# The first microseconds of a windowed attention and its feed-forward layer: masks, reciprocals and values prepared in another way, in another order

## The chip, the cores and the metric

The kernel runs on one core of a Trainium2 chip. A core has a matmul engine (TensorE, PE in the profile, with its weight loads shown apart as PEld), a vector engine (VectorE, DVE), an engine for functions of one operand (ScalarE, ACT), a general engine (GpSimd, POOL) and an engine that only issues transfers (SyncE, SP). Each engine works through its own instructions in the order in which they are written; between engines, semaphores make an instruction wait for its inputs and for the space of its output. 16 DMA engines move data between the memory of the chip (HBM) and the core's memory (SBUF); matmuls write to a second memory, PSUM, of eight banks.

The metric is the time of one execution on the chip, in microseconds (us), lower is better.

## The reference

```python
# q, k, v: 8 batches, 8 heads, 576 positions, 64 wide; w_in 512 x 2048, w_out 2048 x 512
scores = (q @ k.T) / 8
scores = np.where(abs(i - j) <= 32, scores, -1e9)     # a window of 65 keys
attn = np.exp(scores - scores.max(-1)); attn = attn / (attn.sum(-1) + 1e-9)
x = (attn @ v), heads side by side                     # 4608 tokens x 512
h = x @ w_in; g = np.maximum(0.01 * h, h)
out = g @ w_out
```

The maximum is not subtracted in the kernel, since the scores are small. The division by the sum is done after the product with v.

## The kernel before

**Steps.** Heads are taken in pairs: head 0 of a pair lies in partitions 0 to 63, head 1 in 64 to 127. A step is one pair `p` and one half `hf` of a batch `b`: 288 query positions. Step `i` has `b, hf, p = i // 8, (i // 4) % 2, i % 4`; there are 64. The keys are cut into nine blocks of 64 positions, and a half touches five of them (`WIN`, L134): scores come transposed, keys in partitions, queries along the free axis. Even and odd blocks are kept apart in two rows of 288, so that 2 x 288 scores stand in PSUM (`ps`).

A step is made of these parts: `score` (matmuls into ps), `exps` (ACT, L312, the exponential of all 576 columns, to `e` in bf16), `masked` (L320, e times a 0/1 mask on DVE or POOL, to `prob`), `sums` (L342, a matmul with `ones_bd`, which adds the keys of each head and gives the sum in all 64 partitions of that head), `inverse` (L352, reciprocal on DVE), `product` (L367 for batch 0, L375 for the others, prob with v, to `x` in PSUM) and `scaled` (L391, x times the reciprocal, to `xT` in bf16, which is laid out as the next matmul wants it). For batches 1 to 7 the two heads of a pair are put into the diagonal blocks of 128 x 128 matrices (`kbd`, `vbd`), the other blocks being zero, so that one matmul does both heads; vbd has two buffers, for even and odd batches, and the zeros are written once, in the loop of L664 to L668. For batch 0 each head has its own 64 x 64 matmul, from `v0b`.

**Groups.** The steps of one half of a batch (four pairs) make one group of 288 tokens. For it, the first feed-forward matmul (L405) makes 16 tiles `f` of 128 hidden units, each from four chunks `c` (one for each pair); ACT applies the leaky maximum (L416, Prelu) into `gT`. The second (L463) makes the output in tiles of 128 tokens.

**Order.** The order of all instructions is written by hand; a framework only adds the semaphores and the buffers of the tile pools. From batch 1 on, a planner (L716 to L754) spreads the steps between the matmuls of the feed-forward layer by due times. The opening, batch 0 with groups 0 and 1, is a list of calls (L537 to L673). There, `transpose_first` (L208) turns k and q by 18 matmuls for a pair, `evict_first` copies the result to SBUF (L143 on DVE, L141 on ACT), `h_chunk(c)` does chunk c of the first four tiles of group 0, `h_open(f)` does a whole tile f of it, `h_close(f)` is its Prelu. After the list comes group 1 (`h_first(1)`, then L665) and the transposes of batch 1.

In the list before, score(0) stands behind the transposes of k of pair 1. Masks 0 and 1 are made on DVE, 2 to 7 on POOL; every step has its `inverse` on DVE. score(1) to score(6) come ahead of h_chunk(0), score(7) after h_chunk(1).

**Buffers in PSUM.** `mmps` has four banks for everything called `mm` or `tp`: transposes and feed-forward tiles, used in turn. `ps` takes two banks, and `s` and `x` one each: a new score waits until exps has read the last, and so on.

**Masks.** `win` (128 x 128) holds the band of ones, made for each half of the partitions by two selections on POOL (L151, L155: a selection keeps elements where an affine function of partition and column is not negative, and fills the others with 0). `spread` copies it side by side into `wide`, from which the masks are read as overlapping views (`mask_at`).

**Loads.** k and q of batch 0 are loaded by POOL's DMA queue (L99), which converts f32 to bf16, for each pair in turn; v of pair 0 by SP and ACT in f32, then copied to v0b (`value_first`); v of the other pairs by POOL (L116), then w_in in four quarters (L529), w_out in four (L533), and k, q and v of batch 1. POOL issues each of them, which takes it 0.5 to 0.8 us, in one order with its own computations.

**Zero matmuls.** `keep_busy` (L475) issues matmuls of 224 columns of zeros, whose results nobody reads; 14 of them open the program.

Of the kernel before, what the change touches and what calls it, by code (L numbers as in the profile page):

```python
# [9 lines left out]
FP32 = mybir.dt.float32  # L10
# [6 lines left out]
def kernel(  # L17
# [14 lines left out]
    nc = tc.nc  # L32
# [71 lines left out]
    v0b = const.tile([128, NPAIR, NB, D], BF16, name="v0b")  # L104
# [4 lines left out]
    def load_v(b, p, engs=(nc.sync, nc.sync)):  # L109

        cast = engs[0] is nc.gpsimd
        if not cast:
            vf[b, p] = fload.tile([128, NB, D], FP32, name=f"vf{p}")
        for a, r in enumerate(HEADS):
            to = vf[b, p][r] if not cast else v0b[r, p] if b == 0 else vbd[b % 2][r, p, :, r]
# [12 lines left out]
    ident = const.tile([128, 128], BF16)  # L128
# [18 lines left out]
    win = const.tile([128, 128], BF16)  # L147
    nc.gpsimd.memset(win, 1.0)
    for lo in (0, 64):
        w = win[lo:lo + 64]  # L150
        nc.gpsimd.affine_select(  # L151
            out=w, in_=w, compare_op=ALU.is_ge, fill=0.0,
            base=0, channel_multiplier=-1, pattern=[[1, 128]],
        )
        nc.gpsimd.affine_select(  # L155
            out=w, in_=w, compare_op=ALU.is_ge, fill=0.0,
            base=2 * W, channel_multiplier=1, pattern=[[-1, 128]],
        )

# [23 lines left out]
    nc.vector.tensor_copy(out=ident, in_=ident_f)  # L183
# [36 lines left out]
    def value_first(b, p, eng):  # L220
        copy_to(eng, v0b[:, p], vf[b, p])
# [111 lines left out]
    def sums(i):  # L333

        b, hf, p = where(i)
        pr, both = probs[i][:2]
        s = xps.tile([128, HALF], FP32, name="s")
        if both is not None:
            nc.tensor.matmul(s, ones_bd, both, start=True, stop=True)  # L339
        else:  # L340
            for n in range(2):
                nc.tensor.matmul(  # L342
                    s, ones_bd, pr[:, n].rearrange("p c i -> p (c i)"),
                    start=(n == 0), stop=(n == 1),
                )
        probs[i][2] = s
        if b > 0:
            inverse(i)
# [5 lines left out]

    def product(i):
# [7 lines left out]
        if b == 0:  # L363
            for n_, blk, i0, n in parts:
                lo, hi = 2 * i0, 2 * (i0 + n)
                for r in HEADS:
                    nc.tensor.matmul(  # L367
                        x[r, lo:hi], v0b[r, p, blk], flat[r, n_, lo:hi],
                        start=(blk == parts[0][1]), stop=(blk == parts[-1][1]),
                        skip_group_check=True,  # L370
                    )
        else:
            for n_, blk, i0, n in parts:
                lo, hi = 2 * i0, 2 * (i0 + n)
                nc.tensor.matmul(  # L375
                    x[:, lo:hi] if b < NATURAL else x_v[:, :, i0:i0 + n], vbd[b % 2][:, p, blk, :],
                    flat[:, n_, lo:hi] if b < NATURAL else pr[:, n_, :, i0:i0 + n],
                    start=(blk == parts[0][1]), stop=(blk == parts[-1][1]),
                    skip_group_check=True,
                )  # L380
        probs[i][3] = x
# [6 lines left out]

    def scaled(i):
        r, x = probs.pop(i)[2:]  # L390
        nc.vector.tensor_mul(place(i), x, r)  # L391
# [145 lines left out]
    keep_busy(ps, 0, 14, True)  # L537
    fill(V)
    transpose_first(0, 0, "k")
    evict_first(0, 0, "k", V)  # L540
    transpose_first(0, 0, "q")
    evict_first(0, 0, "q", A)
    transpose_first(0, 1, "k")
    score(0)
    evict_first(0, 1, "k", V)
    spread(A, GAP + 32, 2)
    load_v(0, 1, (G, G))
    transpose_first(0, 1, "q")
    exps(0)
    value_first(0, 0, V)  # L550
    transpose_first(0, 2, "k")
    evict_first(0, 1, "q", A)
    spread(V, 0, 3)
    masked(0, V)
    load_v(0, 2, (G, G))
    transpose_first(0, 2, "q")
    evict_first(0, 2, "k", V)
    sums(0)
    evict_first(0, 2, "q", A)
    score(1)  # L560
    inverse(0)
    transpose_first(0, 3, "k")
    exps(1)
    load_v(0, 3, (G, G))
    transpose_first(0, 3, "q")
    evict_first(0, 3, "k", A)
    score(2)
    product(0)
    evict_first(0, 3, "q", A)
    load_w_in(0, 512)  # L570
    masked(1, V)
    exps(2)
    scaled(0)
    sums(1)
    load_w_in(512, 1024)
    score(3)
    inverse(1)
    product(1)
    masked(2, G)
    exps(3)  # L580
    score(4)
    masked(3, G)
    exps(4)
    scaled(1)
    sums(2)
    product(2)
    inverse(2)
    score(5)
    load_w_in(1024, 1536)
    exps(5)  # L590
    masked(4, G)
    score(6)
    scaled(2)
    sums(3)
    h_chunk(0)
    load_w_in(1536, 2048)
    exps(6)
    inverse(3)
    h_chunk(1)
    masked(5, G)  # L600
    score(7)
    product(3)
    h_chunk(2)
    load_w_out(0)
    scaled(3)
    sums(4)
    exps(7)
    h_chunk(3)
    inverse(4)
    masked(7, G)  # L610
    product(4)
    h_close(0)
    h_close(1)
    h_open(4)
    load_w_out(1)
    h_close(2)
    h_open(5)
    scaled(4)
    h_close(4)
    sums(5)  # L620
    masked(6, G)
    h_open(6)
    h_close(3)
    inverse(5)
    h_close(5)
    h_open(7)
    h_close(6)
    product(5)
    load_w_out(2)
    h_close(7)  # L630
    h_open(8)
    h_open(9)
    load_w_out(3)
    h_close(8)
    scaled(5)
    sums(6)
    h_close(9)
    h_open(10)
# [3 lines left out]
    load_first(1, 2, "q", 2)  # L642
    inverse(6)
    product(6)
    h_close(10)
    h_open(11)
# [3 lines left out]
    h_close(12)  # L650
    scaled(6)
    sums(7)
    h_close(13)
    h_open(14)
    inverse(7)
    h_open(15)
    h_close(14)
# [125 lines left out]
```

## Time and profile before

| | us |
|---|---|
| median of 3 runs | 315.69 (315.33 to 316.57) |
| the profiled execution, its own time | 316.52 |
| its span, first to last instruction | 314.8 |
| PE busy | 303.4 (96%) |
| DVE busy | 218.0 (69%) |
| ACT busy | 167.8 (53%) |
| POOL busy | 186.3 (59%) |
| mean granted clock of PE | 0.989 |

The span is what the profile shows; the execution's own time has 1.7 us around it. In the profile's lines, `out<-in` names the tile written and the tile read, `x` and a number is a count, and a bracket at the end of a line of the timeline gives the idle time before it and what ended it. The granted clock is the share of the full clock that PE was given. A transfer's time to landing counts from the start of its issue. "Releaser" is what a waiting instruction waited for last.

Some durations that the prediction uses, in us: reciprocal of 128x288 f32 on DVE 1.956; scaling (L391) 0.457; eviction of 128x576 on DVE 0.756, on ACT 0.650; exps 0.648; Prelu of 128x288 f32 (L416) 0.410; POOL's mask 1.27; DVE's mask 0.51 (median 0.459); memset of 128x576 words on DVE 0.538, of 128x1152 bf16 on POOL 1.108.

Landings of the opening's loads, from the view of transfers: k and q of pair 0 at 4.9 and 5.9, of pair 1 at 7.85 and 8.6, of pair 2 at 9.3 and 10.1, of pair 3 at 10.9 and 11.6; the quarters of w_in at 18.9, 21.5, 24.8 and 27.3, of w_out at 29.8, 32.7, 35.2 and 37.8; the first keys of batch 1 at 39.2.

### The profile page before, as it was taken

Reading aid. Unit: us, or ns where it says so; the run is one execution under the profiler, and the core shown is the slowest. Engines: PE = TensorE matmul, PEld = TensorE weight load, DVE = VectorE, ACT = ScalarE, POOL = GpSimd, SP = SyncE. Lnnn points to the kernel's source line nnn. Section 1 sums busy time; section 2 is a strip of 40 time slices with the busy share of each in tenths; the row PEclk is TensorE's granted clock in tenths of the full one; section 3 lists DMA queues with packets and bytes.
Section 4 is the critical chain, followed back from the end, with each engine's and each line's share of the span. In section 5 each row is a group of like instructions: output and inputs, shape, how many; then the busy total and the mean of one; then the engine's idle time right before and its main releaser. Section 6 shows DMA issues by size and latency. Waiting matters only on the chain.

```text
span 314.8 us, 6932 instructions
## 1 busy us (share of the span) xinstructions
PE 303.4 (96%) x2693; PEld 203.9 (65%) x2714; DVE 218.0 (69%) x268; ACT 167.8 (53%) x370; POOL 186.3 (59%) x257
## 2 busy tenths in 40 slices
PE   4889999999999999999999999999999999999996
PEld 3656755685856767585856758585765858576653
DVE  2889759899647996698655996688655997565100
ACT  2646655482825648282834828284652828364531
POOL 8989975606557855796466856786546866330000
PEclk9779999999999999999999999999999999999999
DMA  8999999969998994599627994699734620000102
GB/s 127 141 185 207 207 149 252 210 145 228 229 199 211 234 196 111 124 201 225 147 56 195 184 225 129 78 248 217 159 77 121 110 55 35 34 35 1 67 28 74
DMA packets 107313, 46.09 MB, mean 146 GB/s; under 512 B 68752, under 2 KB 102800, under 8 KB 107280
## 3 DMA queue, kind: packets, MB, share of 16 engines
q1 hardware_dynamic: 91936, 37.91, 57.9%
q0 software_dynamic: 14752, 7.59, 18.3%
q8 instruction: 21, 0.34, 0.5%
q10 hardware_dynamic: 592, 0.15, 0.2%
q14 instruction: 12, 0.10, 0.1%
HBM read 36.70 MB, written 9.44 MB: 147 GB/s over the span
## 4 chain that ended last, share of the span: by engine, by line
PE 93%; DVE 2%; DMA 2%; POOL 1%; issue 1%; ACT 0%; ACTq 0%; DVEq 0%; POOLq 0%
PE mm L405 40%; PE mm L463 39%; PE x L375 4%; PE ps L301 4%; PE s L339 2%; DVE r L352 2%; DMA qb<-in_q_dram 2%; PE s L342 1%; PE tp L208 1%; PE ps L293 1%; PE x L367 1%; POOL kb L99 0%; PE ps L284 0%; POOL qb L99 0%; ACT e L312 0%
## 5 line engine op out<-in xcount | busy, mean ns | idle before, releaser
L352 DVE RECIPROCAL r<-s 128x288 f32<-128x288 f32 x64 | 125.2, 1956 | 52.9 <-PE s L339 50.6
L405 PE MATMUL mm<-xT,w_in_bf 128*128 128x288 bf16 x1024 | 134.8, 287 | 0.1
L463 PE MATMUL mm<-w_out_bf,gT 128*128 128x512 bf16 (+2 forms) x571 | 129.8, 373 | 1.2 <-issue 0.2
L416 ACT ACTIVATE gT<-mm 128x288 bf16<-128x288 f32 x256 | 101.6, 410 | 26.2 <-PE mm L405 9.3
L405 PEld LDWEIGHTS <-w_in_bf 128*128 128x128 bf16 x1024 | 98.7, 98 | 25.5 <-issue 0.3
L320 POOL TENSOR_TENSOR prob<-e,mask 128x576 bf16<-128x576 bf16 x48 | 61.1, 1272 | 84.1 <-issue 40.2
L463 PEld LDWEIGHTS <-gT 128*128 128x128 bf16 x592 | 55.9, 98 | 57.7
L468 ACT ACTIVATE o_sb<-mm 128x512 f32<-128x512 f32 (+2 forms) x37 | 21.7, 586 | 90.3 <-PE mm L463 90.3
L312 ACT ACTIVATE e<-ps 128x576 bf16<-128x576 f32 x64 | 41.5, 648 | 17.6 <-PE ps L301 7.4
L391 DVE TENSOR_TENSOR xT<-x,r 128x288 bf16<-128x288 f32 x64 | 29.3, 457 | 7.6 <-PE x L367 0.6
L235 POOL CAST vbd<-vf 64x576 bf16<-64x576 f32 x48 | 33.0, 688 | 1.4
L262 DVE COPY kbd<-kT 64x576 bf16<-64x576 bf16 x48 | 32.0, 666 | 0.3
L230 POOL CAST kb<-kf 96x384 bf16<-96x384 f32 x48 | 27.3, 593 | 1.1 <-DMA kf<-in_k_dram 1.1
L230 POOL CAST qb<-qf 96x384 bf16<-96x384 f32 x48 | 24.6, 539 | 4.3 <-DMA qf<-in_q_dram 4.3
L375 PE MATMUL x<-prob,vbd 128*128 128x96 bf16 (+1 forms) x280 | 22.5, 211 | 0.0
L330 DVE TENSOR_TENSOR both<-prob 128x288 bf16<-128x288 bf16 x52 | 19.6, 376 | 0.8
L301 PEld LDWEIGHTS <-kbd 128*128 128x128 bf16 x240 | 15.5, 98 | 6.8
L375 PEld LDWEIGHTS <-vbd 128*128 128x128 bf16 x280 | 17.9, 98 | 2.3
L301 PE MATMUL ps<-qT,kbd 128*128 128x128 bf16 (+2 forms) x240 | 19.3, 211 | 0.0
L339 PE MATMUL s<-both,ones_bd 128*128 128x288 bf16 x52 | 14.9, 286 | 0.0
L320 POOL TENSOR_TENSOR prob<-e,wide 128x576 bf16<-128x576 bf16 x7 | 8.9, 1274 | 4.6 <-ACT e L312 4.5
L141 ACT ACTIVATE qT<-tp 128x576 bf16<-128x576 bf16 x7 | 4.4, 650 | 6.9 <-PE tp L208 6.9
(51 smaller groups left out, 108.7 us busy)
## 6 DMA issues: line engine op xcount, KB each, us to landing
out_dram<-o_sb SPq DMA_DIRECT2D x35, 256.0 KB, 3.7
vf<-in_v_dram SPq DMA_DIRECT2D x49, 144.0 KB, 3.3
qf<-in_q_dram SPq DMA_DIRECT2D x24, 288.0 KB, 4.4
kf<-in_k_dram SPq DMA_DIRECT2D x24, 288.0 KB, 4.7
w_in_bf<-in_moe_w_in_dram POOLq DMA_DIRECT2D x4, 512.0 KB, 8.3
w_out_bf<-in_moe_w_out_dram POOLq DMA_DIRECT2D x4, 512.0 KB, 9.3
kb<-in_k_dram POOLq DMA_DIRECT2D x4, 144.0 KB, 4.9
qb<-in_q_dram POOLq DMA_DIRECT2D x4, 144.0 KB, 5.1
```

Source lines behind the costliest of these rows:

```text
L230: nc.gpsimd.tensor_copy(out=dst[:, p, 3 * c:3 * c + 3], in_=by_c[c])
L235: nc.gpsimd.tensor_copy(out=vbd[b % 2][r, p, :, r], in_=vf[b, p][r])
L262: nc.vector.tensor_copy(out=to.rearrange("p n (m c) -> p n c m", c=2), in_=kT[r].rearrange("p (c n m) -> p n c m", c=2, n=NB),)
L301: nc.tensor.matmul(ps_v[:, n_, :, i0:i0 + n], kbd[b % 2][:, p, blk], by_c[:, :, hf * EVEN + i0:hf * EVEN + i0 + n], start=True, stop=True,)
L312: nc.scalar.activation(out=e, in_=ps[:, P0:P0 + 2 * HALF], func=AF.Exp, scale=scale)
L320: eng.tensor_mul(pr.rearrange("p n c i -> p n (c i)"), e.rearrange("p (n t) -> p n t", n=2), allowed,)
L352: nc.vector.reciprocal(r, probs[i][2])
L375: nc.tensor.matmul(x[:, lo:hi] if b < NATURAL else x_v[:, :, i0:i0 + n], vbd[b % 2][:, p, blk, :], flat[:, n_, lo:hi] if b < NATURAL else ...
L391: nc.vector.tensor_mul(place(i), x, r)
L405: nc.tensor.matmul(h[:, 0:HALF], w_in_bf[:, c, ts(f, 128)], xT[:, c, ds(g * HALF % RING, HALF)], start=(c == 0), stop=(c == DMC - 1),)
L416: nc.scalar.activation(out=to, in_=x, func=AF.Prelu, alpha=0.01)
L463: nc.tensor.matmul(o[:, lo:hi], gT[:, f, ds(128 * j % RING, 128)], w_out_bf[:, f, lo:hi], start=(f == 0), stop=(f == FFC - 1),)
```

## The change

It touches only the opening and what the opening shares with the rest.

1. `band` (128 x 192) takes the place of `win`. Two selections over all 128 partitions make a band from which head 0 reads columns 0 to 127 and head 1 columns 64 to 191; `spread` works on one head at a time. The ones are written by DVE. The identity is made in bf16 directly, its zeros by DVE.
2. For steps 0 to 3 the reciprocal 1/s is made as y = exp(-ln s) on ACT (`log_of`, `guess`) and one Newton step on DVE: `missed` makes s*y, `mended` makes (s*y - 2)*y, which is minus the reciprocal, and `scaled` multiplies by it and by -1. Steps 4 to 7 of batch 0 and all later ones keep the reciprocal of DVE. An ACT table set is named at the start of ACT's queue.
3. v of batch 0 goes into the diagonal blocks of vbd[0], and `product` uses 128 x 128 matmuls there too. vbd[0] is zeroed by DVE at the start; in the loop of group 1 POOL zeroes only vbd[1].
4. The zero matmuls at the start write a tile of mmps instead of ps, and nine more stand between the steps, into a tile `spare`. The sums of steps 1 and 2 go into tiles of mmps as well.
5. The list of the opening is ordered anew: score(0) before the transposes of pair 1, masks 2, 3 and 7 on DVE, evictions dealt out otherwise, three quarters of w_in and most of w_out issued before POOL's first mask, scores 5 to 7 after h_chunk(0).

The core of the diff. Of the old list only the head is shown; it is printed whole above.

```diff
     load_v(0, 0, (nc.sync, nc.scalar))
+    nc.scalar.preload_act_table_set("natural_log_exp_and_others")
     load_first(0, 0, "k")
     load_first(0, 0, "q")
-    ident_f = const.tile([128, 128], FP32)
-    make_identity(nc, ident_f)
-    for p in range(1, NPAIR):
+    ident = const.tile([128, 128], BF16)
+    band = const.tile([128, 64 + 128], BF16)
+    nc.vector.memset(ident, 0.0)
+    nc.vector.memset(band, 1.0)
+    make_identity(nc, ident, nomemset=True)
+    load_first(0, 1, "k")
+    nc.gpsimd.affine_select(
+        out=band, in_=band, compare_op=ALU.is_ge, fill=0.0,
+        base=0, channel_multiplier=-1, pattern=[[1, 192]],
+    )
+    nc.gpsimd.affine_select(
+        out=band, in_=band, compare_op=ALU.is_ge, fill=0.0,
+        base=2 * W, channel_multiplier=1, pattern=[[-1, 192]],
+    )
+    load_first(0, 1, "q")
+    for p in range(2, NPAIR):
...
-    def spread(eng, lo, n):
+    def spread(eng, lo, n, a):
+        r = HEADS[a]
         copy_to(
-            eng, wide[:, lo:lo + 128 * n].rearrange("p (u x) -> p u x", u=n),
-            win.unsqueeze(1).to_broadcast([128, n, 128]),
+            eng, wide[r, lo:lo + 128 * n].rearrange("p (u x) -> p u x", u=n),
+            band[r, 64 * a:64 * a + 128].unsqueeze(1).to_broadcast([64, n, 128]),
         )
...
+    for p in range(NPAIR):
+        nc.vector.memset(vbd[0][:, p], 0.0)
...
-    def value_first(b, p, eng):
-        copy_to(eng, v0b[:, p], vf[b, p])
+    def value_first(a, eng):
+        r = HEADS[a]
+        copy_to(eng, vbd[0][r, 0, :, r], vf[0, 0][r])
...
-    def sums(i):
+    def sums(i, spare=False):
...
-        s = xps.tile([128, HALF], FP32, name="s")
+        if spare:
+            s = mmps.tile([128, 512], FP32, name="mm", tag="mm")[:, 0:HALF]
+        else:
+            s = xps.tile([128, HALF], FP32, name="s")
...
+    def log_of(i):
+        guesses[i] = recip.tile([128, HALF], FP32, name="y")
+        nc.scalar.activation(out=guesses[i], in_=probs[i][2], func=AF.Ln)
+
+    def guess(i):
+        nc.scalar.activation(out=guesses[i], in_=guesses[i], func=AF.Exp, scale=-1.0)
+
+    def missed(i):
+        r = recip.tile([128, HALF], FP32, name="r")
+        nc.vector.tensor_mul(r, probs[i][2], guesses[i])
+        probs[i][2] = r
+
+    def mended(i):
+        r = probs[i][2]
+        nc.vector.scalar_tensor_tensor(
+            out=r, in0=r, scalar=2.0, in1=guesses.pop(i), op0=ALU.subtract, op1=ALU.mult,
+        )
...
+    NEWTON = (0, 1, 2, 3,)
...
+        if i in NEWTON:
+            nc.vector.scalar_tensor_tensor(
+                out=place(i), in0=x, scalar=-1.0, in1=r, op0=ALU.mult, op1=ALU.mult,
+            )
+        else:
+            nc.vector.tensor_mul(place(i), x, r)
...
-    keep_busy(ps, 0, 14, True)
     fill(V)
+    keep_busy(mmps.tile([128, 512], FP32, name="mm", tag="mm"), 0, 14, True)
...
-            nc.gpsimd.memset(vbd[2 - f // 4][:, f % 4], 0.0)
+            if f < 8:
+                nc.gpsimd.memset(vbd[1][:, f % 4], 0.0)
```

The new list, several calls to a line, up to the point where only the order of closes and opens differs:

```python
fill(V); keep_busy(..., 14); spread(V, 0, 3, 0); spread(A, GAP + 32, 2, 0); value_first(0, V)
spread(A, GAP + 32, 2, 1); transpose_first(0, 0, "k"); spread(A, 0, 3, 1); evict_first(0, 0, "k", V)
value_first(1, A); transpose_first(0, 0, "q"); evict_first(0, 0, "q", A); load_v(0, 1, (G, G))
score(0); transpose_first(0, 1, "k"); exps(0); transpose_first(0, 1, "q"); evict_first(0, 1, "k", A)
masked(0, V); load_v(0, 2, (G, G)); evict_first(0, 1, "q", V); product(0); sums(0)
transpose_first(0, 2, "k"); log_of(0); score(1); load_w_in(0, 512); evict_first(0, 2, "k", V)
transpose_first(0, 2, "q"); guess(0); exps(1); load_v(0, 3, (G, G)); transpose_first(0, 3, "k")
missed(0); evict_first(0, 2, "q", A); masked(1, V); transpose_first(0, 3, "q"); mended(0)
evict_first(0, 3, "k", A); sums(1, True); scaled(0); score(2); load_w_in(512, 1024); log_of(1)
evict_first(0, 3, "q", V); product(1); exps(2); load_w_in(1024, 1536); guess(1)
spare = mmps.tile(...); keep_busy(spare, 0, 4, True); score(3); masked(2, V); load_w_in(1536, 2048)
missed(1); sums(2, True); exps(3); mended(1); load_w_out(0); log_of(2); keep_busy(spare, 0, 2, False)
score(4); masked(3, V); guess(2); load_w_out(1); scaled(1); sums(3); exps(4); missed(2); product(2)
mended(2); log_of(3); keep_busy(spare, 0, 3, False); h_chunk(0); load_w_out(2); scaled(2); guess(3)
h_chunk(1); masked(4, G); missed(3); score(5); product(3); mended(3); exps(5); h_chunk(2); scaled(3)
load_w_out(3); sums(4); h_chunk(3); inverse(4); masked(5, G); product(4); h_close(0); score(6)
h_close(1); h_open(4); exps(6); h_open(5); scaled(4); h_close(2); sums(5); masked(6, G)
load_first(1, ...) four times; score(7); h_close(4); inverse(5); product(5); ...
exps(7); h_open(9); scaled(5); h_close(7); sums(6); masked(7, V); h_open(10); ...; inverse(6); ...
```

More of the change, by code (lines that the diff above doesn't have):

```diff
@@ L543 @@
     transpose_first(0, 1, "k")
[L544 to L547, printed above, removed]
+    exps(0)
     transpose_first(0, 1, "q")
[L549 to L553, printed above, removed]
+    evict_first(0, 1, "k", A)
     masked(0, V)
     load_v(0, 2, (G, G))
-    transpose_first(0, 2, "q")
[L557 to L561, printed above, removed]
@@ L562 @@
-    transpose_first(0, 3, "k")
+    evict_first(0, 1, "q", V)
+    product(0)
+    sums(0)
+    transpose_first(0, 2, "k")
+    log_of(0)
+    score(1)
+    load_w_in(0, 512)
+    evict_first(0, 2, "k", V)
+    transpose_first(0, 2, "q")
+    guess(0)
     exps(1)
     load_v(0, 3, (G, G))
+    transpose_first(0, 3, "k")
+    missed(0)
+    evict_first(0, 2, "q", A)
+    masked(1, V)
     transpose_first(0, 3, "q")
+    mended(0)
     evict_first(0, 3, "k", A)
+    sums(1, True)
+    scaled(0)
@@ L567 @@
     score(2)
[L568 to L571, printed above, removed]
+    load_w_in(512, 1024)
+    log_of(1)
+    evict_first(0, 3, "q", V)
+    product(1)
     exps(2)
-    scaled(0)
-    sums(1)
-    load_w_in(512, 1024)
+    load_w_in(1024, 1536)
+    guess(1)
+    spare = mmps.tile([128, 512], FP32, name="mm", tag="mm")
+    keep_busy(spare, 0, 4, True)
     score(3)
-    inverse(1)
-    product(1)
-    masked(2, G)
+    masked(2, V)
+    load_w_in(1536, 2048)
@@ L580 @@
+    missed(1)
+    sums(2, True)
     exps(3)
+    mended(1)
+    load_w_out(0)
+    log_of(2)
+    keep_busy(spare, 0, 2, False)
     score(4)
-    masked(3, G)
+    masked(3, V)
+    guess(2)
+    load_w_out(1)
+    scaled(1)
+    sums(3)
     exps(4)
-    scaled(1)
-    sums(2)
+    missed(2)
     product(2)
-    inverse(2)
+    mended(2)
+    log_of(3)
+    keep_busy(spare, 0, 3, False)
+    h_chunk(0)
+    load_w_out(2)
+    scaled(2)
+    guess(3)
+    h_chunk(1)
+    masked(4, G)
+    missed(3)
@@ L588 @@
     score(5)
-    load_w_in(1024, 1536)
+    product(3)
+    mended(3)
     exps(5)
[L591 to L602, printed above, removed]
     h_chunk(2)
-    load_w_out(0)
     scaled(3)
+    load_w_out(3)
     sums(4)
-    exps(7)
     h_chunk(3)
     inverse(4)
-    masked(7, G)
+    masked(5, G)
     product(4)
     h_close(0)
+    score(6)
     h_close(1)
@@ L642 @@
     load_first(1, 2, "q", 2)
+    score(7)
+    h_close(4)
+    inverse(5)
+    product(5)
+    h_close(3)
+    h_open(6)
+    h_close(5)
+    h_open(7)
+    h_close(6)
+    h_open(8)
+    exps(7)
+    h_open(9)
+    scaled(5)
+    h_close(7)
+    sums(6)
+    masked(7, V)
+    h_open(10)
+    h_close(9)
     inverse(6)
+    h_close(8)
+    h_open(11)
+    h_close(10)
     product(6)
-    h_close(10)
-    h_open(11)
     h_open(12)
```

83 lines of the change are left out of this document (24 added, 59 removed).

## The prediction

> **What bounds the kernel now.** I read the page's busy shares first, then the chain that ended last, then that chain in order of time for the first 60 us.
>
> ```profile
> span 314.8 us, 6932 instructions
> ...
> PE 303.4 (96%) x2693; PEld 203.9 (65%) x2714; DVE 218.0 (69%) x268; ACT 167.8 (53%) x370; POOL 186.3 (59%) x257
> ...
> PE 93%; DVE 2%; DMA 2%; POOL 1%; issue 1%; ACT 0%; ACTq 0%; DVEq 0%; POOLq 0%
> ```
>
> The chain in order of time (start, length, what):
>
> ```profile
> 11.38 1.96 DVE r L352
> ...
> 14.14 1.97 DVE r L352
> ...
> 22.85 1.97 DVE r L352
> ...
> 34.16 6.04 PE mm L405 x48
> ```
>
> PE holds 93% of the chain. Only the opening is not PE's: there the chain goes through loads, then through the reciprocals (L352). PE cannot be helped elsewhere, so the change is worth what it moves the start of PE's unbroken stretch, plus what it saves inside that stretch.
>
> The view of engine busy time in stretches of 3.41 us (columns: stretch, its length, busy us of PE, weight loads, DVE, ACT, POOL, then granted clock, DMA share, GB/s) shows the clock. I chose the borders where the granted clock changes.
>
> ```profile
> 4.27:7.68 3.41, 1.04 (x37) 0.72 (x36) 1.06 (x2) 0.65 (x1) 3.16 (x8) 1.00 1.14 153
> 7.68:11.09 3.41, 3.09 (x84) 2.72 (x84) 2.32 (x5) 1.81 (x4) 3.40 (x6) 0.50 1.28 171
> 11.09:14.50 3.41, 2.65 (x89) 2.08 (x89) 3.18 (x5) 2.73 (x5) 3.19 (x5) 1.00 1.81 119
> 14.50:17.92 3.42, 1.76 (x43) 1.12 (x37) 3.32 (x3) 1.74 (x3) 3.41 (x4) 1.00 1.14 166
> 17.92:21.33 3.41, 3.14 (x22) 1.80 (x23) 2.96 (x3) 0.87 (x2) 3.39 (x4) 0.50 1.09 175
> ```
>
> Stretches in which PE was busy 1.04 and 1.76 us are followed by half clock; the one with 2.65 us (78%) is not. In the second half-clock stretch the first eight L405 matmuls took 2.13 us; eight at full clock take 1.14 to 1.16. So the clock costs 1.0 there.
>
> The timeline of DVE in 14.50 to 17.92 is full (3.32 us): reciprocals. Reciprocals start at 11.38, 14.14, 16.62, 19.48 for steps 0 to 3 and at 22.85, 25.32, 27.99, 30.66 for 4 to 7; the last scaling ends at 33.19, and the 48 L405 matmuls of group 1 (L665) follow and end at 40.2, where the transposes of batch 1 begin (40.13).
>
> **The change, part by part.**
>
> *Before the first score.* POOL loses the memset of win and four selections (6.30 to 7.93), and the identity's memset (0.23); it gets two selections of 128x192 between the loads of k1 and q1. A 128x128 selection took 0.29; a 192-wide one lies between 0.29 and 0.44 (in proportion); I take 0.37. So k1 is issued at 2.9 (was 3.15), band is ready at 4.25, q1 goes out at 4.25 (was 3.70), q3 at 6.4 (was 5.78), the first value load at 6.95 (was 7.93). The loads before it queue for DMA: the six after q0 landed 7.85, 8.6, 9.3, 10.1, 10.9, 11.6, at most 0.82 apart while issued 0.52 apart, so I leave them there; if issue decides, 0.5 later.
> DVE gets memsets: identity, band (0.1 to 0.3 each, nearest the 0.11 to 0.30 of L179 and L224) and four 128x576 halves of vbd (0.54 each, L667), over by 4.3. The fill no longer waits for the zero matmuls, which now write another PSUM tile. Then DVE does half of wide (0.35) and of v (0.45), ACT three quarter copies (0.42 to 0.50) and half of v (0.65). DVE is free at 5.45, ACT at 6.4; the transposes of k0 and q0 end at 5.45 and 6.43 as now. All this costs nothing; without the cover the ACT part is 0.3 late at most.
>
> *Score 0* stood behind the transposes of k1, which waited for their load until 7.93. Now it stands before them: 7.17 instead of 8.43, exps 0 at 7.65 (was 9.12), masked 0 done at 8.9 (was 10.61). But step 1 still needs q1 (8.6), its eviction (DVE 0.76, after the transposes at half clock 0.69) and k1: score 1 at 11.0, was 11.27. So most of the 1.3 us ends there.
>
> *Reciprocals 0 to 3.* Each 1.96 on DVE becomes two ACT passes and two DVE passes. The logarithm reads 128x288 f32: the nearest row is L416's 128x288 f32 at 0.41, the upper bound L312's 0.65; I take 0.41, twice 0.82. The multiply reads one operand from PSUM like L391: 0.46. The Newton step has both inputs in SBUF in f32: between L330 (0.33, bf16, both SBUF) and L391 (0.46); I take 0.40. The scaling stays an L391 (0.46). DVE: 0.86 for 1.96, so 4.4 saved over four steps. In latency 0.41+0.41+0.46+0.40 with four handovers of 0.04 is 1.84, about the same; the gain is that DVE is free for others during the ACT passes.
> DVE's work from the eviction of k0 (5.49) to reciprocal 4: before, evictions 2.27, value and spread 0.80, masks 0.86, reciprocals 7.82, scalings 1.83: 13.6. After: four evictions 3.03, four masks 1.72 (2 and 3 come over from POOL), multiplies 1.83, Newton steps 1.6, scalings 1.83: 10.0. That is 3.6 less.
>
> *Walk forward* (each operation after its inputs and its engine's previous one, 0.04 between; loads as they landed): scalings of steps 0 to 3 end at 13.7, 17.1, 18.6, 20.0; before 14.0, 16.7, 19.1, 22.5. Step 1 is not earlier (DVE does q3's eviction and two masks first), steps 2 and 3 are. Reciprocal 4 starts at 20.1 (22.85). From there steps 4 to 7 run at their old pitch (2.47 to 2.67) plus mask 7, now DVE's (0.46): scaling 7 ends at 30.75 (33.19), 2.4 earlier.
>
> *PE's own account gives the same.* The first w_in matmul: sums 3 at 16.65, product 2 at 17.15, three zero matmuls, then 17.7 (was 19.24): -1.5. Scores 5 and 6 fall behind it instead of before it (0.36 each in the chain): +0.7. Products as five 128x128 matmuls take 0.24 in the chain (L375) against 0.36 (L367) for ten 64x64: five products, -0.6. Clock kept at full: -1.0. Sum -2.4. The nine zero matmuls are 224 columns each, 0.095 at L405's rate (288 in 0.123): 0.86, six of them in waits; the last three (0.29) are in the 17.7. Sums 1 and 2 and the zero matmuls take buffers of the tile mm; so the fourth tile of the first w_in matmuls waits until multiply 2 has read its sums (17.6), which ends beside the zero matmuls.
>
> *Loads.* w_in's first quarter is issued at 10.0 (12.30); with the 6.6 from issue to landing that it took, it is there at 16.6 (18.9), before 17.7. The value loads of pair 3 now follow it: issued at 10.8 and 11.5, 0.6 each behind it, 17.8, used by product 3 at 19.0. POOL issues the rest back to back, so the pauses between landings (w_in 2 came 3.3 after w_in 1, w_out 1 2.9 after w_out 0, the usual is 2.55) go, 1.1 in all; batch 1's first keys, which landed 39.2, 0.9 before their use, land near 37.1. They are then needed at 37.7. This slack of 0.6 is what is late next; it caps the gain near 3.0.
>
> *POOL later* saves four memsets (1.01 pitch) at 31 to 39; the q and k loads of batch 2 behind it come earlier. That meets batch 1's last loads, which have over 1.5 of slack. Nothing on the path.
>
> Sum: -2.4. The profiled execution took 316.52 (span 314.8, 1.7 around it), which gives 314.1; it is 0.8 above the median of the runs, 315.69, so against that **313.3**.
>
> **A rule against it.** DVE operations with two SBUF inputs stood still while POOL worked:
>
> ```profile
> 50.92 0.95 POOL L230 CAST kb<-kf 96x384 bf16<-96x384 f32 x2 [0.37 <-DMA kf<-in_k_dram]
> 51.38 0.80 DVE L320 TENSOR_TENSOR prob<-e,wide 128x576 bf16<-128x576 bf16 x1 [0.62 <-ACT e L312]
> ```
>
> The mask of 0.39 took 0.80 and ended 0.3 after the cast. The Trainium skill (SBUF — State Buffer, Who interferes with whom) says that such an operation and a POOL operation that reads SBUF lock each other out for the whole instruction, whichever started first; by that rule, the trace agrees.
>
> **Rivals.**
> *The Newton step meets POOL's mask.* In my walk Newton step 2 is ready at 17.65 and POOL's mask 4 (1.27) starts at 17.45, after exps 4. If the mask is first, the step waits 1.1; multiply 3 slips, Newton step 3 then meets mask 5 and loses about 0.9 more. Reciprocal 4 starts at 22.0, 0.9 before its old time: 314.8. For it: the rows above. Against it: 0.2 us decides, and if the step is first POOL waits 0.4 at no cost.
> *The clock falls again.* From 14.50 to 17.92 I count PE busy 2.6 of 3.42 (score 3, sums 2, zeros, score 4, sums 3, product 2, zeros), near the 2.65 that kept it and above the 1.76 that did not; only the zero matmuls make the difference. If it falls, 1.5 of the gain goes: 314.8.
> *The loads hide it.* If the loads of q1 to q3 come 0.5 later and the stream after them gains nothing, batch 1's keys land at 39.2 still: PE gains 0.9, 314.8.
> *Slower: the logarithm reloads ACT's tables.* The trace has one table load (1.28) for copy, exp and Prelu together; none shows the logarithm. Four logarithms between exps cost up to eight loads, 10.3, on an ACT that has 8.5 of work (five exps, three evictions, eight passes) in some 10 us there: 8.8 lost, 2.4 won, 322. Two extra loads would already cancel the gain. Against it: the change names one set ahead of everything. The Trainium skill (ScalarE: Activation LUTs, Table sets: the hidden batching unit) lists a set with both exp and ln, which no run here shows.
> *Slower: POOL stalls issuing.* At 29.5 seven loads were outstanding without a longer issue; the change has nine or so by 17. If POOL then waits until w_in 2 lands (23), mask 4 ends at 24.5, reciprocal 4 starts near 25: 318. It turns slower once mask 4 ends after 22.2.
>
> **Numbers.** Forecast 0.45; lock-out 0.20; clock 0.15; loads 0.08; tables 0.05; POOL stall 0.07. A measurement of this kernel tells 0.5% (1.6 us) from no change. The forecast's own range is 312.3 to 314.2 (the Newton step at 0.33, ACT passes overlapping, up to 3.4 gained; handovers longer, 1.5). The three middle rivals lie at 314.4 to 315.8. The range takes them: 312.3 to 316.0; outside stay the slower two (0.12) and some 0.05 below. Faster by over 0.5%: 0.44 of the forecast and 0.06 of the rivals' better ends, 0.50; slower 0.11; same 0.39.
>
> **What would show it.** Right: score 0 near 7.2; no reciprocal before 20; reciprocal 4 at 20.1; w_in's first matmul at 17.7 with granted clock 1.0 from 11 to the end; batch 1's transposes at 37.7; one table load. Wrong: a DVE f32 operation of over 0.8 beside POOL's mask; half clock in 18 to 21; a PE wait on batch 1's keys; a second table load; POOL issues over 1 us.

## The result and the profile after

| | before | after |
|---|---|---|
| median of 15 runs each | 315.80 us | 315.05 us |
| lowest and highest | 314.84, 318.18 | 314.11, 316.34 |
| ratio | | 0.9962 (95% interval 0.9945 to 0.9979) |
| the profiled execution, its own time | 316.52 | 314.20 |
| its span | 314.8 | 312.5 |

The changed kernel is faster by 0.38%, some 1.2 us, with an interval of 0.7 to 1.7; the two medians differ by 0.75. The forecast was 2.4 us. The two profiled executions differ by 2.3 us, as the forecast said, but they are not typical: that of before is 0.7 above its median, that of after 0.85 below.

The page of after, the same lines as were shown of before:

```profile
span 312.5 us, 6890 instructions
...
PE 304.2 (97%) x2662; PEld 205.7 (66%) x2683; DVE 218.7 (70%) x281; ACT 171.4 (55%) x380; POOL 177.9 (57%) x246
...
PE 94%; DVE 2%; DMA 1%; issue 1%; ACT 1%; POOL 0%; DVEq 0%; ACTq 0%; POOLq 0%
```

The chain of after in order of time (start, length, what):

```profile
17.73 0.46 DVE xT L409
18.18 0.37 DVE r L371
18.56 0.02 issue
18.58 0.86 DVE r L376
...
19.53 0.47 DVE xT L409
...
28.52 1.97 DVE r L357
...
31.87 6.04 PE mm L427 x48
37.91 0.69 PE tp L209 x36
```

The reciprocals of steps 0 to 3 are gone from it; multiply (L371), Newton step (L376) and scaling (L409) of steps 1 to 3 stand there, and the chain passes to PE at 20.0. Of the opening's reciprocals only that of step 7 (28.52) is left in it. The 48 matmuls of group 1 start at 31.87 (34.16 before) and batch 1's transposes at 37.91 (40.20). What follows is the same in both: from those transposes to the start of the last ACT instruction it is 271.7 us in before and in after. It is within 0.1 of that in the profile of every experiment below, so all differences between the profiles lie in the opening.

Its busy time in the same stretches as before:

```profile
11.09:14.50 3.41, 3.40 (x83) 2.61 (x77) 2.95 (x6) 2.71 (x6) 3.22 (x6) 1.00 1.84 175
14.50:17.92 3.42, 3.15 (x42) 2.32 (x40) 3.04 (x8) 3.17 (x8) 2.96 (x5) 1.00 1.55 183
17.92:21.33 3.41, 3.29 (x46) 2.29 (x45) 3.27 (x5) 1.38 (x4) 3.21 (x3) 1.00 1.24 207
```

PE is busy 3.15 us from 14.50 to 17.92, where it was 1.76, and ACT 3.17 where it was 1.74. The granted clock reads 1.00 everywhere. The durations say that the clock was not full before 13.5: eighteen transposes take 0.69 until 13.03 and the two matmuls of a sum 0.66, against 0.47 and 0.41 at full clock. In this profile and in that of before once more, below, the reading is 1.00 although the first matmuls run at half speed.

### The profile page after: what moved, and what is told of

It is laid out like the page before. It is cut to its first block, busy times and chain, and to the rows that moved or that the text cites. A ratio compares the mean times of both kernels' runs of the same rounds, so it can differ in the third digit from the quotient of the medians.

```text
span 312.5 us, 6890 instructions
## 1 busy us (share of the span) xinstructions
PE 304.2 (97%) x2662; PEld 205.7 (66%) x2683; DVE 218.7 (70%) x281; ACT 171.4 (55%) x380; POOL 177.9 (57%) x246
## 3 DMA queue, kind: packets, MB, share of 16 engines
q1 hardware_dynamic: 91936, 37.91, 61.7%
## 4 chain that ended last, share of the span: by engine, by line
PE 94%; DVE 2%; DMA 1%; issue 1%; ACT 1%; POOL 0%; DVEq 0%; ACTq 0%; POOLq 0%
PE mm L485 40%; PE mm L427 39%; PE x L390 5%; PE ps L303 4%; PE tp L209 2%; PE s L344 2%; DMA qb<-in_q_dram 1%; PE s L347 1%; PE ps L286 1%; DVE r L357 1%; PE ps L295 1%; DVE r L376 1%; DVE xT L409 0%; DVE r L371 0%; ACT e L314 0%
## 5 line engine op out<-in xcount | busy, mean ns | idle before, releaser
L357 DVE RECIPROCAL r<-s 128x288 f32<-128x288 f32 x60 | 117.4, 1956 | 52.3 <-PE s L344 50.3
L314 ACT ACTIVATE e<-ps 128x576 bf16<-128x576 f32 x64 | 41.4, 647 | 13.8 <-PE ps L303 7.4
L413 DVE TENSOR_TENSOR xT<-x,r 128x288 bf16<-128x288 f32 x60 | 27.5, 458 | 6.4 <-DVE r L357 0.5
L390 PE MATMUL x<-prob,vbd 128*128 128x128 bf16 (+2 forms) x320 | 26.0, 213 | 0.0
L390 PEld LDWEIGHTS <-vbd 128*128 128x128 bf16 x320 | 20.3, 98 | 2.9
L115 POOL DMA_DIRECT2D vbd<-in_v_dram x14 | 10.4, 757 | 4.7 <-DMA kb<-in_k_dram 2.2
L322 DVE TENSOR_TENSOR prob<-e,wide 128x576 bf16<-128x576 bf16 x12 | 5.8, 485 | 4.1 <-ACT e L314 4.0
```

Of the source, the lines that this page charges most:

```text
L314: nc.scalar.activation(out=e, in_=ps[:, P0:P0 + 2 * HALF], func=AF.Exp, scale=scale)
L322: eng.tensor_mul(pr.rearrange("p n c i -> p n (c i)"), e.rearrange("p (n t) -> p n t", n=2), allowed,)
L357: nc.vector.reciprocal(r, probs[i][2])
L390: nc.tensor.matmul(x[:, lo:hi] if b < NATURAL else x_v[:, :, i0:i0 + n], vbd[b % 2][:, p, blk, :], flat[:, n_, lo:hi] if b < NATURAL else ...
```

## The experiments

The theories: **clock** (the forecast's 1.0 us was earned against one execution of before that had two half-clock stretches), **lock-out** (Newton step 3 waits for POOL's mask 4), **loads** (transfers now land just in time, and their scatter is passed on), and for the gain itself **reciprocal** (work taken from DVE) against **order** (earlier scores, earlier loads).

Each experiment was timed beside runs of before, and each ratio is against these. In the text below, the *stretch* is the time from the first w_in matmul to batch 1's first transposes, read from the timeline of PE: 20.89 us in before (19.24 to 40.13), 20.50 in after (17.34 to 37.84).

**The kernel before once more**, unchanged.

> The kernel before, unchanged, with the span and granted clock of each run. Theory clock: its profiled run (316.52, mean clock 0.989, which is two half-clock stretches of 3.41 us) was one of its slower runs; runs with a mean clock of 0.994 (one stretch) or more take about 315.2, so that the clock term of 1.0 us in the forecast was gained against that run and is worth half or less against the median. Theory loads: clock and time are not related here, all runs lie near a clock of 0.989, and what fell short lies in the changed kernel.

Median 315.74 beside 316.33 of before, ratio 0.9988 (0.9969 to 1.0008). Over all experiments there are 136 runs of before, these included: 75 show a mean granted clock of 0.998 or more and take 315.83 on average, 61 show less and take 316.80. The profiles agree on what half clock costs when it falls on the first w_in matmuls. In before:

```profile
19.24 2.13 PE L405 MATMUL mm<-xT,w_in_bf 128*128 128x288 bf16 x8
...
40.13 0.75 PE L208 MATMUL tp<-ident,kb 64*64 64x64 bf16 x36
```

and in before once more, which ran at full clock from 14 on:

```profile
19.15 1.14 PE L405 MATMUL mm<-xT,w_in_bf 128*128 128x288 bf16 x8
...
39.38 0.76 PE L208 MATMUL tp<-ident,kb 64*64 64x64 bf16 x36 [0.19 <-DMA kb<-in_k_dram]
```

The five profiles of the old order split in the same way: where those eight matmuls took 2.12 or 2.13, the stretch is 20.88 to 20.91 (before and, further down, the Newton path in the old order and before with early keys); where they took 1.14, it is 20.23 and 19.96 (before once more, before with zero matmuls). So the price, 0.7 to 1.0, was near the forecast's, but the kernel before shows a lower clock in 45% of its runs only: 0.44 on average.

In after 10 of 15 runs show 0.998 or more (314.79), 5 less (315.48). If that difference is the clock's, the changed kernel still pays 0.23, and the term is worth 0.2; if it is not, 0.4. The profiles don't show it to be the clock's: in five of the eleven that have the new order and the Newton path the reading is below 1.00, always between 7.7 and 14.5, where the others run at half clock too, unrecorded, until 11.3 to 13.8 by the lengths of their transposes and sums; and none has half clock after 14.5. The term is worth 0.2 to 0.4, not 1.0.

In before once more, the opening meets something else at its end:

```profile
26.70 12.63 DMA kb<-in_k_dram
39.33 0.04 issue
39.38 0.76 PE tp L208 x36
```

These are the lines of its chain: the transposes were released by the load of batch 1's first keys, and PE stood idle for 0.19. The early half clock seems to cost little: this execution ran at half clock until 14, that of before was at full clock at 5 and from 11 on, and their first w_in matmuls start 0.09 apart.

**Before with zero matmuls**, and **after with one instead of nine**.

```diff
+    spare = mmps.tile([128, 512], FP32, name="mm", tag="mm")
     score(4)
+    keep_busy(spare, 0, 5, True)
...
     score(5)
+    keep_busy(spare, 0, 6, False)
```

> The kernel before with eleven zero matmuls of 224 columns added in idle time of TensorE, five after score 4 and six after score 5, and nothing else. Theory clock: the stretch at 14.5 to 17.9 gets about 1 us more of matmul time (2.8 of 3.4), the half-clock stretch at 18 to 21 goes, mean clock 0.994 or more, and the time falls by 0.3 to 1.0. Theory loads: TensorE then waits for reciprocals or w_in anyway, and the time stays within 0.3 of before.

Median 316.15, ratio 0.9994 (0.9977 to 1.0011); 8 of 12 runs at 0.998 or more.

```diff
-    keep_busy(spare, 0, 4, True)
+    keep_busy(spare, 0, 1, True)
...
-    keep_busy(spare, 0, 2, False)
...
-    keep_busy(spare, 0, 3, False)
```

> The changed kernel with one of its nine later zero matmuls instead of nine. Theory clock: TensorE's busy time from 14.5 to 17.9 falls by 0.7, half clock follows in more of the runs, mean clock below 1.0 in most, and the time rises by 0.5 to 1.5 over the changed kernel. If the zero matmuls do nothing, clock and time stay within 0.2 of the changed kernel.

Median 314.95, ratio 0.9956 (0.9939 to 0.9973); 7 of 12 at 0.998 or more. Neither moves the time by more than the intervals, some 0.5 us, and the share of runs with full clock does not move beyond what a dozen runs can tell. The zero matmuls are worth nothing that these runs can see. That the clock would fall without them did not come about: with one of them, the profile has no half clock after 14.5 either.

**Batch 1's first keys earlier.** They change places with the last quarter of w_out in POOL's queue.

```diff
-    load_w_out(3)
+    load_first(1, 0, "k", 2)
     sums(4)
...
     masked(6, G)
-    load_first(1, 0, "k", 2)
+    load_w_out(3)
```

> The changed kernel with the first keys of batch 1 issued where the last quarter of w_out stood, and that quarter behind them; so these keys land some 2.5 us earlier and the quarter 1.4 later. Theory loads: in the changed kernel the transposes of batch 1 start at 37.9, level with the landing of those keys, so that slower loads are passed on to the end; with the keys early the median falls by 0.4 to 0.8, to 314.4, and the spread shrinks. Theory clock: no change, 315.0 within 0.2.

Median 315.13, ratio 0.9965 (0.9947 to 0.9984): nothing gained. The profiles show what else was late. In the timeline of the version with one zero matmul:

```profile
17.82 0.75 POOL L555 DMA_DIRECT2D w_out_bf<-in_moe_w_out_dram  x1 [1.13 <-DMA w_in_bf<-in_moe_w_in_dram]
17.86 0.45 DVE L371 TENSOR_TENSOR r<-s,y 128x288 f32<-128x288 f32 x1
18.35 1.85 DVE L376 SCALAR_TENSOR_TENSOR r<-r,y 128x288 f32<-128x288 f32 x1
18.58 1.29 POOL L322 TENSOR_TENSOR prob<-e,wide 128x576 bf16<-128x576 bf16 x1
...
20.30 0.46 DVE L409 SCALAR_TENSOR_TENSOR xT<-x,r 128x288 bf16<-128x288 f32 x1
```

and in that of after:

```profile
17.05 0.75 POOL L555 DMA_DIRECT2D w_out_bf<-in_moe_w_out_dram  x1 [0.45 <-DMA w_in_bf<-in_moe_w_in_dram]
17.16 0.46 DVE L376 SCALAR_TENSOR_TENSOR r<-r,y 128x288 f32<-128x288 f32 x1
...
17.81 1.29 POOL L322 TENSOR_TENSOR prob<-e,wide 128x576 bf16<-128x576 bf16 x1
...
18.58 0.85 DVE L376 SCALAR_TENSOR_TENSOR r<-r,y 128x288 f32<-128x288 f32 x1
```

Newton step 3 takes 0.85 in after and 1.85 with one zero matmul instead of 0.46, and 1.64 with early keys, and each time it ends 0.33 after POOL's mask 4. The lock-out is there, in step 3 rather than in step 2, because POOL comes to mask 4 late: all four quarters of w_in and three of w_out are issued ahead of that mask, and POOL stands 0.45 to 1.13 us until w_in's first quarter has landed before it can issue w_out 2. The Trainium skill (SBUF — State Buffer, Who interferes with whom) says that a DVE operation with two SBUF inputs and a POOL operation that reads SBUF exclude each other; the trace agrees on the wait. It says that the one that starts first goes first; by the recorded starts the step of 1.85 began 0.23 before the mask and still waited. POOL's recorded spans are rough, so this is left open.

**Reciprocals of steps 0 to 3 on DVE again**, in the new order.

```diff
-    log_of(0)
...
-    guess(0)
...
-    missed(0)
+    inverse(0)
...
-    mended(0)
```

and so for steps 1 to 3, with `NEWTON = ()`.

> The changed kernel with VectorE's reciprocal for steps 0 to 3 again, at the place of the multiply; logarithm, exponential and Newton step are gone. Theory reciprocal (VectorE's work in the opening sets its end, and the Newton path takes 3.6 us of it away): reciprocal 4 starts 1.5 to 3 us later than 20.0, the median is 316.5 to 318, slower than the kernel before. Rival order (the gain lies in the order and the earlier loads): within 0.5 of the changed kernel.

Median 317.66, ratio 1.0043 (1.0026 to 1.006): 2.6 above after, and slower than before. The first w_in matmul comes at 19.20; after three of them PE stands until 20.54, when reciprocal 2 (18.54 to 20.50) has read the sums whose PSUM tile the fourth needs. Reciprocal 4 starts at 23.43 (19.96 in after). Its chain is one of DVE:

```profile
16.09 1.87 DVE r L357
...
18.63 1.88 DVE r L357
...
21.05 1.88 DVE r L357
...
23.02 0.47 DVE xT L413
```

**The Newton path in the old order**, nothing else changed.

```diff
-    inverse(0)
+    log_of(0)
+    guess(0)
+    missed(0)
+    mended(0)
```

and so for steps 1 to 3, with the table set named and the scaling of the change.

> The kernel before, in its old order, with only the reciprocals of steps 0 to 3 replaced by logarithm, exponential and Newton step at the place of the reciprocal. Theory reciprocal: reciprocal 4 starts 1 to 2 us earlier than 22.85 and the time falls by 0.7 to 1.5. Rival order: the chain of one step is no shorter (1.8 against 1.96 us), so without the new order the time falls by less than 0.3, or rises, since ScalarE's extra passes stand ahead of exps.

Median 316.71 beside 316.28, ratio 1.0017 (0.9999 to 1.0034): no gain. In its profile, which has half clock at the first w_in matmuls, multiply 1 waits 1.05 and multiply 2 waits 1.03 for ACT, and Newton step 2 takes 2.00 beside POOL's mask of step 4; it ends 0.9 after that mask, and why it took longer here than in the new order is open. So neither half gains alone, where the new order stands for all the rest of the change: masks, loads, products and list, which were not taken apart further. The new order without the Newton path loses 0.43%, the Newton path without the order gains nothing that shows, and both together gain 0.38%. That the order matters because it gives DVE other work during ACT's two passes fits these waits, but is argued, not shown.

**Products of batch 0 by 64x64 matmuls again**, on the diagonal blocks of vbd[0].

```diff
+        for n_, blk, i0, n in parts if b == 0 else ():
+            lo, hi = 2 * i0, 2 * (i0 + n)
+            for r in HEADS:
+                nc.tensor.matmul(
+                    x[r, lo:hi], vbd[0][r, p, blk, r], flat[r, n_, lo:hi],
...
-        for n_, blk, i0, n in parts:
+        for n_, blk, i0, n in parts if b > 0 else ():
```

> The changed kernel with ten 64x64 matmuls for each product of batch 0 again, on the diagonal blocks of the same tile. By the forecast's term (0.12 us for each of the five products in TensorE's unbroken stretch) the time rises by 0.5 to 0.7. If the products run beside other waits, within 0.2.

Median 315.08, ratio 0.996 (0.9945 to 0.9976), the same as after. Its stretch is 20.62 with a Newton step 3 of 0.84, where after has 20.50 with 0.85: 0.12 for five products by these two profiles, where the forecast had 0.6.

**s*y kept in PSUM.** The multiply writes over s, so that the Newton step has one operand in PSUM.

```diff
     def missed(i):
-        r = recip.tile([128, HALF], FP32, name="r")
-        nc.vector.tensor_mul(r, probs[i][2], guesses[i])
-        probs[i][2] = r
+        s = probs[i][2]
+        nc.vector.tensor_mul(s, s, guesses[i])
...
-        r = probs[i][2]
+        s = probs[i][2]
+        r = probs[i][2] = recip.tile([128, HALF], FP32, name="r")
...
-            out=r, in0=r, scalar=2.0, ...
+            out=r, in0=s, scalar=2.0, ...
```

> The changed kernel with the product s*y written back into PSUM in place of s, so that the Newton step has one input in SBUF and one in PSUM. Theory lock-out: Newton step 3, which took 0.85 instead of 0.46 beside POOL's mask 4, takes 0.46 whatever POOL does; scaling 3 and reciprocal 4 come 0.4 earlier, the time falls by 0.2 to 0.4 to about 314.7. Rival (the step is slow for another reason, its two f32 inputs or the queue): Newton step 3 stays at 0.8 and the time is the same or longer.

Median 314.86, ratio 0.9965 (0.9939 to 0.9991). No Newton step takes more than 0.46 now. How such a step runs beside POOL's mask is seen in a later version, below. But scaling 3 then waits 0.91 for product 3, since the first w_in matmul stood until 17.89 for its quarter, and the transposes of batch 1 wait 0.23 for their keys. The median is 0.2 below that of after, which is within the intervals.

**The first quarter of w_in earlier**, ahead of the values of pair 2; then with s*y in PSUM; then also with mask 4 ahead of w_out 2; then also with the Newton path for steps 4 to 7. The edit of the second is the one above, the fourth has `NEWTON = tuple(range(8))` and the four calls in place of `inverse`; of the other two:

```diff
     masked(0, V)
+    load_w_in(0, 512)
     load_v(0, 2, (G, G))
...
-    load_w_in(0, 512)
```

and, for mask 4,

```diff
-    load_w_out(2)
     scaled(2)
...
     masked(4, G)
+    load_w_out(2)
```

> The changed kernel with the first quarter of w_in issued ahead of the value loads of pair 2. In the profiles so far that quarter landed between 16.8 and 18.2; POOL's issue of w_out 2 waited for it, and POOL's mask 4 behind that issue met Newton step 3 (0.85 to 1.85 instead of 0.46). Theory late quarter (the landing sets both the first w_in matmul and the collision): it lands near 15.5, w_out 2 waits for nothing or for less, mask 4 starts when exps 4 ends (17.2), Newton step 3 takes 0.46 to 0.85, and the time falls by 0.3 to 0.6 to about 314.5. Rival: mask 4 then meets Newton step 2 (17.2) instead and costs the same, or product 2 waits for its values; no gain.

Median 314.97, ratio 0.9964 (0.995 to 0.9979): no gain. The quarter landed near 16.3, but then POOL waits 1.48 at w_out 0 instead of 0.45 at w_out 2, mask 4 starts at 18.76, and Newton step 3 takes 1.41.

> The same with s*y kept in PSUM, so that no Newton step can be locked out. Theory lock-out and late quarter together: both hindrances gone, reciprocal 4 starts near 19.6, the time falls by 0.6 to 1.0 below the changed kernel, to 314.0 to 314.4. If only one of the two matters, it equals that one's run within 0.2.

Median 314.76, ratio 0.9956 (0.9939 to 0.9972), 0.2 below its neighbour without PSUM, again within the intervals. Products 1 and 2 now wait 0.7 in all for the values that the quarter overtook, and the transposes 0.25 for the keys; reciprocal 4 starts at 20.43, not 19.6. Its timeline shows the Newton step with one operand in PSUM beside the mask (start, length, engine, line):

```profile
18.61 1.31 POOL L322 TENSOR_TENSOR prob<-e,wide 128x576 bf16<-128x576 bf16 x1
18.71 0.46 DVE L376 SCALAR_TENSOR_TENSOR r<-s,y 128x288 f32<-128x288 f32 x1
```

The step lies wholly inside POOL's mask 4 and takes its usual 0.46. With both operands in SBUF it ended 0.33 after the mask each time in the new order, so the two SBUF inputs are what made it wait.

> The same as the last, with POOL's mask 4 ahead of the issue of w_out 2. If that issue's wait still holds mask 4, sums 4 and reciprocal 4 come earlier and the time falls by 0.1 to 0.4 more; if the wait has gone with the early quarter, no difference (within 0.2).

Median 314.57, ratio 0.9956 (0.9937 to 0.9974): 0.2 below the last, within the intervals. Mask 4 now ends at 19.05 (19.92 before this step), and reciprocal 4 starts at 20.20 instead of 20.43.

> The same as the last, with the reciprocals of steps 4 to 7 made by logarithm, exponential and Newton step too. VectorE's chain from reciprocal 4 to scaling 7 (11 us in the changed kernel's profile, with TensorE idle 0.4 at its end for scaling 7) gets 1.1 us shorter for each step, and TensorE's own work bounds that stretch: 0.3 to 0.8 off, to 313.5. Rival: ScalarE's extra 0.8 us a step delays the Prelu passes that free TensorE's PSUM tiles; then no gain or a loss of up to 0.5.

Median 314.53, ratio 0.9942 (0.9922 to 0.9961), on five runs: the fastest version, 0.6% below before and 0.2% below after, whose interval it overlaps. The 313.5 that was expected did not come: TensorE's wait of 0.36 for scaling 7 is gone, but its profile has waits of 0.18 and 0.23 for ACT's Prelu in its place.

The profiles of these versions bound the lock-out's price. The longest Newton step and the stretch: 0.84 and 20.62, 0.85 and 20.50, 1.41 and 20.89, 1.64 and 21.02, 1.85 and 21.02; with no lock-out 20.71 and 20.65, of which 0.23 and 0.25 were spent on the keys, 20.40 and 20.42. So a step of 0.85 goes with 0.2 at most, and the longer ones with some 0.5. These are single profiles of versions that differ in other things too; the medians show no more than 0.2 for the lock-out's removal. Three of the five profiles in which it can occur have 1.4 or more; that of after, with 0.85, is among the two that lose little by it.

**Both hindrances away, and before with early keys.**

> The changed kernel with s*y kept in PSUM (no lock-out) and with batch 1's first keys issued ahead of the last quarter of w_out. In the profile with s*y in PSUM alone, TensorE stood 0.23 us for these keys at 38.6; with the keys early alone, the lock-out took 1.2. Theory loads next: with both hindrances gone, the median is 0.3 to 0.6 below either run alone, near 314.4. Rival: the landing of w_in's first quarter and of the values sets the stretch, and the pair gives no more than 0.2.

Median 315.05, ratio 0.998 (0.9957 to 1.0004): no gain, and a wide scatter (313.89 to 318.49). Its profiled run shows a third load on the path:

```profile
21.33 0.43 PE L286 MATMUL ps<-qT,kT 64*64 64x64 bf16 x10
23.07 1.15 PE L427 MATMUL mm<-xT,w_in_bf 128*128 128x288 bf16 x8 [1.30 <-DMA w_in_bf<-in_moe_w_in_dram]
```

The second quarter of w_in landed at 23.0 here, and PE stood for it 1.3 us.

> The version with all eight reciprocals of batch 0 by Newton step, early first quarter of w_in and mask 4 ahead of w_out 2, now with batch 1's first keys early too. Theory loads next: 0.2 to 0.5 below 314.5. Rival: no wait on keys is left in that version (its profile shows none), within 0.2.

Median 314.62, ratio 0.9962 (0.9944 to 0.9979): no gain over the version without.

> The kernel before with batch 1's first keys issued ahead of the last quarter of w_out. In its profile with full clock TensorE stood 0.19 us for these keys at 39.4, in that with half clock it came 0.9 after them. Theory loads next: the runs with full clock gain 0.1 to 0.3, the median 0.0 to 0.2. If the kernel before were held by its loads in most runs, it would gain 0.5 or more.

Median 315.59, ratio 0.9995 (0.9979 to 1.0011): the kernel before is not held by those keys to a degree that shows.

## Why the prediction was wrong

**The walk held for the profiled execution.** In the profile of after, with the forecast in brackets: score 0 at 7.32 (7.2), first reciprocal on DVE at 19.96 (20.1), first w_in matmul at 17.34 (17.7), scaling 7 ends at 31.05 (30.75), transposes at 37.91 (37.7), one table load of 1.28. The profiled executions differ by 2.3 (2.4). Against its own reference the sum holds, but in part by luck: the first w_in matmul came 1.9 earlier instead of 1.5, the stretch became 0.4 shorter instead of 0.9, and the profiled execution of after, at 314.20, is the second fastest of its 15. In the four versions nearest to after (one zero matmul, early keys, 64x64 products, s*y in PSUM) the transposes start at 38.34 to 38.60.

**The step that failed is the clock's term, with the way from the profile to the median.** "Clock kept at full: -1.0" was read off one execution with two half-clock stretches, and the whole sum was then taken from the median of the runs. Only 45% of the runs of before show a lower clock, and a third of those of after; the term is worth 0.2 to 0.4. Three runs lay on the table and the profiled one was 0.8 above their median: the forecast noted that, and still took the whole 2.4 off the median. Between the runs that read 0.998 or more, the gain is 315.83 - 314.79 = 1.0.

**The products' -0.6 came to about -0.1.** It counted PE as unbroken from the first w_in matmul on. PE is not: it waits for scaling 3, or loads, or scaling 7 (0.36 in the profile of after). That shorter products only lengthen those waits is argued. With the clock at 0.2 to 0.4 and the products at 0.1, the forecast's sum becomes 1.1 to 1.3, beside the 1.2 of the ratio; since its other terms moved too, that fit is no proof that nothing else was wrong.

**The lock-out came true as a rival, at another step.** It was put at Newton step 2 with a chance of 0.20; it is in step 3 in all five profiles of the new order that can have it. The forecast's walk let POOL issue back to back, and gave the stall that it named as a rival no part in this one: POOL stood until w_in's first quarter had landed. The price is some 0.5 by the longest cases, not 1.5.

**The loads.** Where it kept its place, the first quarter landed between 16.8 and 17.8 in the profiles (forecast 16.6), k of pair 2 at 10.1 in after instead of 9.3, the keys of batch 1 at 37.5 in after and at 37.0 to 38.6 where they were not issued earlier (37.1). The forecast named these keys as what is late next and had 0.6 of slack; after has 0.3, and in two profiles PE waited 0.23 and 0.25 for them. No single load explains the rest: earlier keys, an earlier quarter and no lock-out moved the median by 0.2 at most one by one, and in seven of the eleven profiles PE waited for a load, in changing places. That the scatter of landings makes up the rest is argued, not shown.

**Tables and POOL's stall.** One table load, no issue over 0.9: neither slow rival came about, but the stall did in small, as waits of 0.45 to 1.7 between issues.

## What to carry to other kernels

Before a term is taken from one profile, ask in how many runs its cause occurs: a clock that falls in half of the runs is worth half, and where the profiled execution lies off the median, the difference is a part of the sum. When several things are just in time, count a saving only up to the next late thing, and list those: here a scaling, a mask and four loads took turns. A change of operation and a change of order can be worth nothing apart and something together; undo each alone before crediting either.

## What the runs showed of the hardware

- The granted clock can read 1.00 at the start where matmuls run at half speed: 18 transposes took 0.69 us until 13.03 in the profile of after under a reading of 1.00, 0.47 at full clock. The durations tell.
- POOL stood before issuing a load three times when eight of its loads had not landed: until 10.39 (the keys of pair 2), until 17.05 (w_in's first quarter) and until 36.58 (w_out's last), by counting issues and landings in the profile of after. Whether program or chip sets that number, these runs don't tell. In before, no more than seven were out when an issue began.
- A multiply that writes over its PSUM input took 0.46, as one that writes to SBUF (0.45), and with one operand in PSUM the Newton step runs under POOL's mask in 0.46, where with two in SBUF it took 0.84 to 1.85, ending 0.33 after the mask (2.00 in the old order, ending 0.9 after it).
- A logarithm of 128x288 f32 out of PSUM took 0.41 and the exponential behind it 0.44, with a Prelu of the same size at 0.41, all with one table load of 1.28 at the start.
